# First loads on one queue, modulation columns by halves of the output, eleven GpSimd normalising steps and a new written-out order, in a block of local attention and a token-mixing MLP

## The chip, the core and the metric

The program runs on one core of a Trainium2 chip. The core has five engines that work side by side and meet through semaphores: TensorE (PE, with its weight loads PEld), VectorE (DVE), ScalarE (ACT), GpSimd (POOL) and SyncE (SP, which here only issues transfers). Sixteen DMA engines move the data. The metric is the device time of one execution in microseconds; lower is better.

## The reference

The input x has 2048 tokens of 512 features, in bfloat16. Six vectors of 512 come out of a small modulation product, and two residual branches use them:

```
mod = silu(c) @ w_mod                       # w_mod: 512 x (6*512)
sa, ca, ga, sb, cb, gb = the six slices of mod
h = layernorm(x) * (1 + ca) + sa
q, k, v = h @ wqkv                          # 32 heads of 16
# each token attends to 8 tokens: itself and 2, 4, ... 14 tokens back
attn = softmax(q . k[s - 2w] * 0.25, w = 0..7)
x = x + ga * ((attn-weighted v) @ wo)
h = layernorm(x) * (1 + cb) + sb
u = gelu(layernorm(h)^T @ w1 + b1)          # mixes along the 2048 tokens, 1792 hidden
x = x + gb * (u @ w2 + b2)^T
```

## The kernel before, in words

Tokens are worked in four chunks of 512 (`build_chunk(ch)`, line 546), each of four tiles of 128 tokens. For a chunk the program takes the row statistics of x (`ln1s`, helper `stats`, line 350), their reciprocal root (`rstd1`, line 360), a helper column -mean/std (`nb1`, `negmean`, line 374) and the normalised rows (`ln1n`, `norm`, line 380). TensorE transposes these into PSUM (`tr`, line 576) and an eviction that multiplies by 1+ca and adds sa writes the transposed activations (`hT`, line 583). Three projections follow (`qkvq`, `qkvk`, `qkvv`, line 608) with their evictions (`evq`, `evk`, `evv`).

The attention of a chunk is elementwise work on VectorE: four products of q with shifted k (`qk`, 4096 columns each, line 651), summed per head on TensorE (`red`), a maximum (`max`), its subtraction on TensorE (`sub`), the exponential on ScalarE (`exp`), the sum over the window on TensorE (`sum`), its reciprocal on ScalarE (`rb`), the scaling on VectorE (`smul`), the spreading of the weights to all lanes on TensorE (`a2`, evicted by `a2ev`), four products of the weights with shifted v (`pv`, 4096 columns each, line 726) and their sums on TensorE (`pvacc`, line 736). The shifted copies of v are made by transfers inside SBUF (`vd`, eight for each half of the head features, into the tiles vD). Then come the output projection (`wo`), its eviction with the residual (`x1ev`), sums of squares (`x1sq`), `rstd2`, `nb2`, the second normalisation (`t`), two VectorE steps with 1+cb and sb (`aff`), the third normalisation (`ln3s`, `rstd3`, `nb3`, `h3`). Where `x1ev` of a tile is on ScalarE, its `wo` has a fifth matmul that adds the residual (line 763).

The MLP's first product runs over tokens. Its first half (tiles 0 to 7) is accumulated in `mlp1_0_..` as those tiles come ready and parked in SBUF (`park0`); the second half is `mlp1_1_..`, joined by `gadd`, `gelu` and `gbm`. The second product (`mlp2`, line 917) gives the output tiles, each finished by one VectorE addition (`fin`) and one store (`st_out`). The last tile, 15, is done in two pieces of 256 columns.

Several steps may run on more than one engine: `add_any` (line 112) holds the alternatives. Which one is taken, and the order of all steps, is written out by hand in the string `ORDER` (line 27): `ln1n4:a` means that step on ScalarE, `:v` on VectorE; a digit is one of the four PSUM slots of two banks each. `schedule` (line 147) reads the string and only refuses an order that breaks a dependency. The numbers beside the alternatives are not read by it. Each engine runs its steps strictly in that order, and so does the SP queue its transfers.

The beginning, which the change touches: `ld_c` (1 KB) and `ld_wmodA` are issued by ScalarE, and `ld_x00`, `ld_x02`, `ld_wmodB`, `ld_x1`, `ld_w1a` and the rest by SP. `ld_wmodA` and `ld_wmodB` (lines 404 and 406) bring the first 1024 columns of w_mod, each for half of the 512 input features, in rows of 2 KB. `silu` is one ScalarE exponential and three VectorE steps (lines 454 to 461). `modcols0` and `modcols1` (line 472) make columns sa and ca, each over half of the inputs, so that both halves of the weights are needed for any column; `modcols_h` and `modcols_cp` add them. `warm0` to `warm4` are matmuls on the identity with no use but to keep TensorE working (line 463, counts in `WARM`, line 246).

Of the kernel before, what the change touches and what calls it, by code (L numbers as in the profile page):

```python
# [13 lines left out]
P = 128  # L14
# [13 lines left out]
consts ld_x00 ld_c consts2 warm2:0 ld_x02 ld_wmodA ld_wmodB act_table ld_x1 warm4:1 ld_w1a ld_w1b ln1s0:v ld_x2 cps:2  # L28
warm0:3 ld_w0 silu_exp ln1s1:a silu_dve halo0 ln1s2:v ln1s3:v rstd1_0_0 modcols0:0 ld_w2 nb1_0_0 rstd1_0_2 warm3:1
ln1n0:v modcols_h ln1n1:a nb1_0_2 ln1n3:v modcols1 ln1n2:v ld_wo1 tr0_00:2 tr0_02 ld_wmod5 modcols_cp tr0_10:3 hT0_0:v  # L30
tr0_12 ln1s7:a warm1:1 hT0_2:v hT0_1:v ld_x3 hT0_3:v qkvk0_0:0 ln1s6:a ln1s5:v qkvk0_0b qkvk0_2:2 ld_wmod2 ln1s4:v
evk0_0:a sc_rep rstd1_1_0 ln1s10:v ld_wo2 qkvk0_1:1 evk0_2:a ld_wo3 nb1_1_0 ln1s11:v qkvq0_0:3 ln1n5:a ln1n7:v
qkvq0_2:0 ln1s8:v evk0_1:a ln1n4:a khalo1 ln1s9:v ld_b1 evq0_0:a ln1n6:v rstd1_2_0 ld_wmod4 qk0_0 tr1_10:2 evq0_2:a
ld_wmod3 tr1_00:1 qkvq0_1:3 hT1_2:a ld_wo0 hT1_0:a qkvv0_0:0 nb1_2_0 qk0_2 hT1_3:a evq0_1:a hT1_1:a qkvv0_2:2 evv0_0:a
qk0_1 ln1n10:a qkvq1_0:3 evv0_2:a ln1n8:v ln1s15:a vd0_020 qk0_3 qkvk1_0:1 vd0_001 vd0_011 evq1_0:a red0_0:0 vd0_021
evk1_0:a ln1s12:v red0_1 vd0_000 red0_2 ln1s14:a ln1n11:v vhalo1 red0_3 qk1_0 vd0_131 qkvk1_2:2 vd0_010 ln1n9:a
vd0_121 ln1s13:a vd0_030 qkvq1_2:3 max0 ld_b2 evk1_2:a qk1_1 sub0 evq1_2:a qkvv1_0:1 khalo2 vd0_031 exp0 vd0_101 qk1_2
rstd1_3_0 vd0_111 sum0 tr2_00:2 vd0_130 rb0 red1_0:3 hT2_0:a vd0_120 red1_1 nb1_3_0 smul0 vd0_110 evv1_0:a red1_2
qk1_3 a2_0:0 vd0_100 hT2_1:a tr2_10:1 a2ev0:a qkvv1_2:2 hT2_2:a pv0_0 ln1n14:a red1_3 hT2_3:a modrows:0 ln1n13:a
qkvq2_0:1 pv0_1 mrow_ev evv1_2:a bc0 ln1n12:a biascols:0 vd1_130 pvacc0_0:2 biascols_cp ln1n15:a max1 pvacc0_1 vd1_021  # L40
evq2_0:a vd1_100 tr3_00:0 pv0_3 vd1_010 sub1 oev0_1:a qkvv2_0:1 vd1_011 exp1 vd1_020 vd1_030 pv0_2 hT3_0:a sum1
vd1_000 qkvk2_0:2 evv2_0:a vd1_001 hT3_1:a vd1_031 gmul rb1 vd1_110 pvacc0_2:1 evk2_0:a pvacc0_3 vd1_120 tr3_10:0
# [5 lines left out]
vd2_131 x1ev7:a vd2_121 ln3s0_0:v red2_0:1 x1sq4 red2_1 vd2_031 ln3s0_2:v red2_2 vd2_111 x1sq7 red2_3 ln3s0_1:v
vd2_001 qkvv3_0:0 x1ev6:a max2 vd2_101 rstd3_0_0 x1sq6 ld_w1_0_0 nb3_0_0 qk3_1 sub2 evv3_0:a qkvq3_2:2 rstd2_1_0 exp2
nb2_1_0 qkvv3_2:3 h3_2:v h3_3:v t7:a h3_1:v h3_0:v t6:a qk3_0 qkvk3_2:0 t5:a ld_w1_0_6 t4:a evv3_2:a sum2 aff1_0 rb2  # L50
red3_0:3 vd3_011 evq3_2:a mlp1_0_10_0:1 vd3_030 vd2_110 evk3_2:a mlp1_0_11_0 smul2 vd3_010 ln3s1_3:a ln3s1_1:v
mlp1_0_30_0:2 ld_w1_0_2 vd2_100 ln3s1_0:v red3_1 ln3s1_2:a vd2_130 mlp1_0_31_0 qk3_2 vd3_031 a2_2:0 vd3_000 rstd3_1_0
vd3_021 a2ev2:a nb3_1_0 vd3_020 red3_2 qk3_3 vd3_001 h3_5:a mlp1_0_00_0:0 h3_7:a mlp1_0_01_0 h3_6:a h3_4:v pv2_0
red3_3 mlp1_0_11_4 mlp1_0_10_4 max3 vd3_120 mlp1_0_31_4 park0_1:a mlp1_0_01_4 pv2_1 sub3 pvacc2_0:1 exp3 mlp1_0_00_4
pv2_2 vd3_101 sum3 vd3_100 pvacc2_1 rb3 vd3_121 mlp1_0_30_4 oev2_1:a vd3_130 smul3 mlp1_0_60_0:3 park0_3:a vd3_110
pv2_3 a2_3:1 ld_w1_0_4 pvacc2_2:2 vd3_111 a2ev3:a mlp1_0_61_0 vd3_131 pv3_0 ld_w1_1_5 pvacc2_3 mlp1_0_60_4 oev2_3:a
ld_w1_0_5 mlp1_0_61_4 park0_0:a pv3_1 wo9:1 park0_6:a wo10:2 wo11:0 x1ev9:v ld_w1_1_3 x1ev10:v wo8:3 x1sq9 x1ev11:v
# [173 lines left out]
def kernel(  # L231
# [35 lines left out]
    def T(shape, dtype, name):  # L267
        return sb.tile(shape, dtype, name=name)
# [695 lines left out]
```

## Time and profile before

| | |
|---|---|
| median of three runs | 200.23 us (200.03 to 200.43) |
| the profiled execution's own time | 199.6 us |
| its span, first to last instruction | 197.9 us |
| TensorE busy | 190.3 us, 1270 matmuls |
| VectorE busy | 156.5 us |
| ScalarE busy | 125.7 us |
| GpSimd busy | 4.3 us, all in the first 6 us |
| granted TensorE clock | 1.00 in every stage |
| DMA, mean | 170 GB/s, 33.58 MB |

All steps are recorded through one helper (line 183), so that rows of the profile are told apart by the tiles that they write and read: `prod`, `gT` and `h` written from `q_sb,k_c` are the `qk` products, `pvb` from `a2sb,vD` the `pv` products, `ps` from `pvb,stack` is `pvacc`, `ps` from `prod,group` is `red`. Times in rows are microseconds from the start of the span, then the duration; where a row ends with `x4` it is four instructions of a kind, from the start of the first to the end of the last. A duration holds the latency too, so that two neighbours on an engine start closer together than one duration; the distance of starts is called the pitch here.

### The profile page before, as it was taken

Reading aid. Unit: us, or ns where it says so; the run is one execution under the profiler, and the core shown is the slowest. Engines: PE = TensorE matmul, PEld = TensorE weight load, DVE = VectorE, ACT = ScalarE, POOL = GpSimd, SP = SyncE. Lnnn points to the kernel's source line nnn. Section 1 sums busy time; section 2 is a strip of 40 time slices with the busy share of each in tenths; the row PEclk is TensorE's granted clock in tenths of the full one; section 3 lists DMA queues with packets and bytes.
Section 4 is the critical chain, followed back from the end, with each engine's and each line's share of the span. In section 5 each row is a group of like instructions: output and inputs, shape, how many; then the busy total and the mean of one; then the engine's idle time right before and its main releaser. Section 6 shows DMA issues by size and latency. Waiting matters only on the chain.

```text
span 197.9 us, 3368 instructions
## 1 busy us (share of the span) xinstructions
PE 190.3 (96%) x1270; PEld 89.4 (45%) x1292; DVE 156.5 (79%) x209; ACT 125.7 (64%) x243; POOL 4.3 (2%) x30
## 2 busy tenths in 40 slices
PE   7999999999999999979999999999999999999994
PEld 2656545444444445424434444444444444444452
DVE  1899999999999999999999999946894515261554
ACT  3799999999999999994777999934732000000000
POOL 7100000000000000000000000000000000000000
DMA  5999965547972589696499999998000069000212
GB/s 189 364 337 325 262 148 123 165 109 177 168 126 50 161 231 230 199 216 139 109 198 271 293 284 296 288 296 227 3 0 0 27 183 297 27 27 27 83 50 82
DMA packets 45331, 33.58 MB, mean 170 GB/s; under 512 B 5252, under 2 KB 42756, under 8 KB 45316
## 3 DMA queue, kind: packets, MB, share of 16 engines
q1 hardware_dynamic: 45036, 32.85, 65.5%
q10 hardware_dynamic: 280, 0.53, 0.7%
q8 instruction: 10, 0.16, 0.4%
q14 instruction: 5, 0.04, 0.1%
HBM read 22.03 MB, written 2.10 MB: 122 GB/s over the span
## 4 chain that ended last, share of the span: by engine, by line
PE 54%; ACT 6%; DVE 4%; DMA 2%; issue 1%
PE ps L183 54%; DVE h L183 2%; DMA vD<-v_c 2%; ACT junk L183 2%; ACT h L183 1%; DVE gT L183 1%; ACT v_c L183 1%; DVE pvb L183 1%; ACT ee L183 1%; ACT a2sb L183 0%; ACT k_c L183 0%; ACT q_sb L183 0%; ACT lv L183 0%; DVE k_c L183 0%; ACT rb L183 0%
## 5 line engine op out<-in xcount | busy, mean ns | idle before, releaser
L183 DVE TENSOR_TENSOR pvb<-a2sb,vD 128x4096 bf16<-128x4096 bf16 x16 | 36.1, 2286 | 0.1
L183 PE MATMUL ps<-h,wst 128*128 128x512 bf16 x123 | 29.0, 379 | 0.6 <-ACT a2sb L183 0.2
L183 DVE TENSOR_TENSOR prod<-q_sb,k_c 128x4096 bf16<-128x4096 bf16 x9 | 20.5, 2287 | 0.3 <-ACT q_sb L183 0.3
L183 PEld LDWEIGHTS <-wst 128*128 128x128 bf16 x128 | 12.0, 98 | 16.6 <-issue 3.2
L183 PE MATMUL ps<-gT,vD 128*128 128x512 bf16 x83 | 19.1, 379 | 0.1
L183 DVE TENSOR_TENSOR q_sb<-ps,q_sb 128x512 bf16<-128x512 f32 x8 | 5.5, 688 | 14.2 <-PE ps L183 13.7
L183 PE MATMUL ps<-woq,o_sb 128*128 128x512 bf16 x61 | 15.3, 379 | 0.2
L183 PE MATMUL ps<-hTb,w_q 128*128 128x512 bf16 x63 | 15.1, 379 | 0.1
L183 PE MATMUL ps<-hTb,w_v 128*128 128x512 bf16 x60 | 14.8, 380 | 0.3
L183 PE MATMUL ps<-hTb,w_k 128*128 128x512 bf16 x62 | 14.9, 380 | 0.1
L183 PEld LDWEIGHTS <-w_q 128*128 128x128 bf16 x96 | 10.2, 108 | 10.6 <-issue 0.8
L183 PEld LDWEIGHTS <-o_sb 128*128 128x128 bf16 x106 | 10.2, 98 | 9.9 <-ACT o_sb L183 0.3
L183 DVE TENSOR_TENSOR k_c<-ps,k_c 128x512 bf16<-128x512 f32 (+1 forms) x9 | 5.6, 629 | 11.0 <-PE ps L183 11.0
L183 PEld LDWEIGHTS <-vD 128*128 128x128 bf16 x116 | 9.3, 97 | 10.4
L183 PEld LDWEIGHTS <-w_v 128*128 128x128 bf16 x80 | 8.5, 111 | 9.5 <-issue 2.3
L183 PE MATMUL ps<-gT,pvb 128*128 128x512 bf16 x53 | 12.6, 379 | 0.2
L183 ACT ACTIVATE junk<-xx,su 128x512 bf16<-128x512 bf16 x16 | 11.6, 722 | 1.6 <-DVE xx L183 1.3
L183 PEld LDWEIGHTS <-w_k 128*128 128x128 bf16 x80 | 8.5, 111 | 8.9 <-issue 1.3
L183 PE MATMUL ps<-gT,prod 128*128 128x512 bf16 x55 | 12.4, 379 | 0.1
L183 ACT ACTIVATE gT<-n_sb,b1col 128x512 bf16<-128x512 f32 x8 | 5.3, 714 | 7.7 <-DVE n_sb L183 7.7
L183 PEld LDWEIGHTS <-ident 128*128 128x128 bf16 (+1 forms) x75 | 6.4, 103 | 7.6 <-issue 2.4
L183 DVE BATCH_NORM_STATS2 st<-xx 128x6 f32<-128x512 bf16 x10 | 6.8, 680 | 3.8 <-DMA xx<-in_A_x_dram 3.8
(109 smaller groups left out, 318.5 us busy)
## 6 DMA issues: line engine op xcount, KB each, us to landing
vD<-v_c SPq DMA_DIRECT2D x64, 131.5 KB, 4.6
wst<-in_B_w_dram SPq DMA_DIRECT2D x8, 512.0 KB, 5.7
vD<-in_B_w_dram SPq DMA_DIRECT2D x3, 896.0 KB, 8.3
wst<-in_w_mod_dram SPq DMA_DIRECT2D x4, 512.0 KB, 10.1
prod<-in_B_w_dram SPq DMA_DIRECT2D x2, 896.0 KB, 8.9
pvb<-in_B_w_dram SPq DMA_DIRECT2D x2, 896.0 KB, 10.1
xx<-in_A_x_dram SPq DMA_DIRECT2D x3, 512.0 KB, 8.5
w_q<-in_B_w_dram SPq DMA_DIRECT2D x2, 512.0 KB, 5.0
```

Source lines behind the costliest of these rows:

```text
L183: r = fn(*a, **k)
```

## The change

It has seven parts.

1. First loads. The modulation weights come as four transfers, all on SP right behind the two loads of x: `ld_wmodA1`, `ld_wmodA0`, `ld_wmodB1`, `ld_wmodB0`, each for all 512 inputs and 256 output columns, in rows of 512 bytes. ScalarE issues a 1 KB load from w_mod into a tile `touch` that nothing reads. `ld_x1` is split in two and stands between the halves of the key weights; `ld_x3` and `ld_b2` move ahead of `ld_w2`.
2. Modulation columns. `modcols0` and `modcols1` each make half of the output columns over all inputs. `modcp0` and `modcp1` copy them out. Transposes are paired so that a PSUM slot holds feature tiles kp and kp+2, and `hT` of tiles 0 and 1 needs only the first half of the columns.
3. `silu` becomes three ScalarE steps (exponential, logarithm of 1 plus it, exponential) and one VectorE product.
4. `WARM` goes from (8, 6, 4, 4, 3) to (4, 4, 2, 3, 3).
5. Eleven normalising steps move to GpSimd: `ln1n6`, `ln1n4`, `ln1n8`, `ln1n11`, `t5`, `t4`, `t7`, `h3_3`, `h3_1`, `h3_11`, `h3_8`. Seven of them were on VectorE; `ln1n4`, `t5`, `t4` and `t7` were on ScalarE.
6. `ORDER` is new throughout, and other steps change between ScalarE and VectorE (among them `hT0_1` to ScalarE, `hT1_1`, `ln1s13`, `h3_6` to VectorE, `h3_2`, `h3_4` and `x1ev11` to ScalarE).
7. The last output tile is cut into 384 and 128 columns.

```
-    WARM=(8, 6, 4, 4, 3),
+    WARM=(4, 4, 2, 3, 3),
...
     def norm(dst, src, rs_ap, nb_ap, reads, nbkey, writes, name, mean_ap=None):
...
         alts = [("dve", _ts4(D, 2), f_dve),
                 ("act", _act(D, 2, False), lambda: nc.scalar.activation(dst, src, ACT.Identity, scale=rs_ap,
-                                                                        bias=nb_ap))]
+                                                                        bias=nb_ap)),
+                ("pool", 0.78, lambda: nc.gpsimd.tensor_scalar(dst, src, rs_ap, nb_ap, op0=ALU.mult, op1=ALU.add))]
...
+    dma(touch[:], w_mod.rearrange("(a b) n -> a b n", b=D // 16)[:, 0, 0:32], 1024, [], ["touch"], "ld_touch", "act")
...
-    dma(wmodA[:, 0:2, :], wmod_view[:, 0:2, 0:2 * D], 2 * D * P * 2 * 2, [], vdk[0][4:], "ld_wmodA", "act")
     G.head = [o.idx for o in G.ops if o.name.startswith("ld_x0")]
-    dma(wmodA[:, 2:4, :], wmod_view[:, 2:4, 0:2 * D], 2 * D * P * 2 * 2, [], vdk[0][:4], "ld_wmodB")
+    for hf in range(2):
+        for v in (1, 0):
+            c0 = v * D + hf * (D // 2)
+            z = 4 - 4 * hf + 2 * v
+            dma(wmodA[:, :, c0:c0 + D // 2], wmod_view[:, :, c0:c0 + D // 2], D * P * 4, [], vdk[0][z:z + 2],
+                f"ld_wmod{'AB'[hf]}{v}")
...
+        for (a, z) in ((0, 2), (2, TPC)) if ch == 1 else ((0, TPC),):
+            dma(xx[:, ch * TPC + a:ch * TPC + z, :], x_view[:, ch * TPC + a:ch * TPC + z, :], (z - a) * P * D * 2, [],
+                [("xx", ch * TPC + i) for i in range(a, z)], f"ld_x{ch}" + ("ab"[a // 2] if ch == 1 else ""))
...
+    def f_sig():
+        nc.scalar.activation(ecol[:], bank(sl_c, 0)[:, 0:KT], ACT.Exp, scale=-1.0)
+        nc.scalar.activation(ecol[:], ecol[:], ACT.Ln, bias=1.0)
+        nc.scalar.activation(ecol[:], ecol[:], ACT.Exp, scale=-1.0)
...
-                for dt_ in range(KT):
-                    for kt in (2 * kh, 2 * kh + 1):
+                for dt_ in (2 * kh, 2 * kh + 1):
+                    for kt in range(KT):
...
+        def f_cp(kh=kh):
+            pm = bank(sl_m, kh)
+            nc.vector.tensor_copy(sacol[:, 2 * kh:2 * kh + 2], pm[:, 2 * kh:2 * kh + 2])
+            nc.vector.tensor_scalar(a1col[:, 2 * kh:2 * kh + 2], pm[:, KT + 2 * kh:KT + 2 * kh + 2], 1.0, None, op0=ALU.add)
...
-                                                n_sb[:, sl, (2 * kp + k2) * P:(2 * kp + k2 + 1) * P], ident[:])
+                                                n_sb[:, sl, (2 * k2 + kp) * P:(2 * k2 + kp + 1) * P], ident[:])
...
-            for (c0, c1) in ([(0, D)] if st < NST - 1 else [(0, D // 2), (D // 2, D)]):
+            for (c0, c1) in ([(0, D)] if st < NST - 1 else [(0, 3 * P), (3 * P, D)]):
```

The pieces of the new order that the prediction speaks of:

```
+silu_exp ln1s0:v ld_w1a ln1s1:a ld_x1a silu_dve ln1s2:v halo0 ld_w1b warm2:3 ld_x1b ln1s3:v rstd1_0_0 ld_x2 modcols0:0
+ld_w0 rstd1_0_2 nb1_0_0 warm3:1 ln1n0:v ld_x3 ln1n1:a modcp0 nb1_0_2 ln1n2:v modcols1 ln1n3:v ld_b2 tr0_00:2 tr0_10:3
+modcp1 tr0_02 sc_rep ld_w2 tr0_12 hT0_0:v warm4:1 hT0_1:a hT0_2:v ld_wo0 ln1s4:a hT0_3:v qkvk0_0:0 ld_wmod2 ln1s7:v
...
+nb1_1_0 ln1s9:v ld_wo3 ln1n6:g ln1n5:a qkvq0_2:1 ln1s10:v evq0_1:a ln1n4:g evk0_2:a qk0_1 ln1n7:a qkvq0_0:3 evk0_0:a
...
+red0_0:3 ln1s13:v ln1n8:g vd0_120 red0_1 evk1_0:a ln1s12:v red0_2 vd0_130 ln1n11:g ln1n10:a red0_3 vd0_021 qk1_0
...
+biascols:0 qkvk3_2:3 ln3s0_2:v vd2_130 rstd2_1_0 ln3s0_0:a nb2_1_0 vd2_020 ln3s0_1:v t5:g qkvq3_2:2 ln3s0_3:v vd2_031
+t4:g t6:a max2 ld_w1_0_2 t7:g evk3_2:a aff1_0 evq3_2:a sub2 qkvv3_2:3 rstd3_0_0 exp2 nb3_0_0 biascols_cp h3_2:a h3_3:g
+sum2 ln3s1_2:v qkvv3_0:2 rb2 h3_1:g ln3s1_3:v ln3s1_0:a h3_0:v smul2 mlp1_0_10_0:0 ld_w1_0_6 qk3_0 evv3_0:a
```

More of the change, by code (lines that the diff above doesn't have):

```diff
@@ L27 @@
 ORDER = """
[L28 to L42, printed above, removed]
@@ L48 @@
[L48 to L57, printed above, removed]
@@ new lines @@
+tr1_10:2 evq0_0:a khalo1 tr1_00:0 hT1_1:v evq0_2:a qkvv0_2:3 ld_wmod3 qk0_0 ld_wmod5 hT1_0:a hT1_3:a qkvv0_0:1 hT1_2:a
+qk0_2 evv0_2:a qkvq1_0:2 evv0_0:a ln1s14:a qk0_3 vd0_131 qkvk1_0:0 vd0_030 vd0_011 rstd1_2_0 evq1_0:a vd0_020 nb1_2_0
+red0_0:3 ln1s13:v ln1n8:g vd0_120 red0_1 evk1_0:a ln1s12:v red0_2 vd0_130 ln1n11:g ln1n10:a red0_3 vd0_021 qk1_0
+qkvq1_2:1 ln1s15:a vd0_001 vd0_000 vd0_010 ln1n9:a qkvk1_2:2 max0 vd0_031 rstd1_3_0 vhalo1 evq1_2:a qk1_1 sub0
+qkvv1_0:0 evk1_2:a exp0 khalo2 qk1_3 vd0_110 tr2_00:1 evv1_0:a sum0 vd0_100 tr2_10:2 rb0 vd0_121 qkvv1_2:0 hT2_0:a
@@ new lines @@
+red3_3 pv2_0 mlp1_0_31_4 mlp1_0_11_4 max3 mlp1_0_10_4 vd3_120 vd3_110 mlp1_0_01_4 park0_1:a pv2_1 vd3_020 sub3 bc3
+pvacc2_0:0 exp3 mlp1_0_30_4 pv2_2 vd3_131 sum3 vd3_011 pvacc2_1 rb3 mlp1_0_00_4 vd3_111 oev2_1:a vd3_121 smul3
+mlp1_0_60_0:3 park0_0:a vd3_130 pv2_3 a2_3:0 vd3_100 mlp1_0_61_0 a2ev3:a vd3_101 ld_w1_0_4 pvacc2_2:2 ld_w1_1_0
+pvacc2_3 pv3_0 mlp1_0_60_4 oev2_3:a mlp1_0_61_4 park0_3:a wo11:0 pv3_1 park0_6:a ld_w1_0_5 wo8:2 x1ev11:a wo10:1
+ld_w1_1_3 x1ev8:v wo9:3 x1ev10:v x1sq8 pvacc3_0:0 ld_w1_1_1 x1sq11 x1ev9:v pvacc3_1 pv3_2 x1sq10 mlp1_0_20_0:2 x1sq9
```

96 lines of the change are left out of this document (46 added, 50 removed).

## The prediction

> **What bounds the kernel now.** I read the page first, then the chain that ended last, then the rows of TensorE and VectorE in the stretches that the chain names, and last the first 17 us.
>
> ```profile
> span 197.9 us, 3368 instructions
> PE 190.3 (96%) x1270; PEld 89.4 (45%) x1292; DVE 156.5 (79%) x209; ACT 125.7 (64%) x243; POOL 4.3 (2%) x30
> PE   7999999999999999979999999999999999999994
> DVE  1899999999999999999999999946894515261554
> ```
>
> The chain (start, length, what) and, behind it, rows of TensorE and VectorE (start, length; in brackets the idle time before and who ended it):
>
> ```profile
> 87.03 0.92 ACT a2sb L183
> ...
> 127.02 10.74 PE ps L183 x49
> ...
> 190.27 4.73 PE ps L183 x28
> ...
> 195.02 0.42 DVE k_c L183
> ```
>
> ```profile
> 64.27 0.62 PE L183 MATMUL ps<-pvb,stack 128*32 128x512 bf16 x8 [0.31 <-DVE pvb L183]
> ...
> 87.16 0.61 PE L183 MATMUL ps<-gT,group 128*32 128x512 bf16 x8 [0.90 <-DVE gT L183]
> ...
> 98.00 6.75 DVE L183 TENSOR_TENSOR pvb<-a2sb,vD 128x4096 bf16<-128x4096 bf16 x3
> ...
> 100.55 0.62 PE L183 MATMUL ps<-pvb,stack 128*32 128x512 bf16 x8
> ```
>
> In the page's slices each digit is a fortieth of the span, 4.9 us, in tenths. From the chain's last ScalarE piece at 87.03 on there is only TensorE, at 219 ns a matmul (10.74 us for 49), to its last matmul near 195.0; then one 0.42 us addition and the last store. VectorE stands at nine tenths or more from the third slice to about 128 us. TensorE looks as full, but its small idle times before 100 us name VectorE products (0.31 and 0.90 us above): it keeps step with VectorE there and only afterwards has a backlog. The hand-over is the last `pv` product of chunk 2, the first of the three that start at 98.00; its `pvacc2_3` starts at 100.55. What lies on TensorE behind it is fixed work. So the end moves with (a) the time at which VectorE finishes that product and (b) TensorE work added behind it. (a) is the time of VectorE's first `qk` product plus the VectorE work between the two plus its waits.
>
> **The start.**
>
> ```profile
> 1.42 3.17 PE L183 MATMUL ps<-ident 128*128 128x512 bf16 x7 [1.42 <-POOL onecol L183]
> ...
> 1.79 0.47 SPq L183 DMA_DIRECT2D vD<-in_w_mod_dram  x1
> ...
> 4.63 2.33 PE L183 MATMUL ps<-ident 128*128 128x512 bf16 x8
> ...
> 8.06 0.54 PE L183 MATMUL ps<-sc,vD 128*128 128x1 bf16 x16
> ...
> 8.47 1.05 PE L183 MATMUL ps<-ident,n_sb 128*128 128x128 bf16 x16
> ...
> 9.07 0.63 ACT L183 ACTIVATE junk<-xx 128x512 bf16<-128x512 bf16 x1 [0.62 <-DMA xx<-in_A_x_dram]
> ...
> 9.11 1.90 DVE L183 TENSOR_SCALAR hTb<-ps,a1col,sacol 128x512 bf16<-128x512 bf16 x4 [0.24 <-PE ps L183]
> ...
> 10.65 3.62 PE L183 MATMUL ps<-hTb,w_k 128*128 128x512 bf16 x15
> 10.68 0.63 ACT L183 ACTIVATE junk<-xx 128x512 bf16<-128x512 bf16 x1
> ...
> 12.15 0.58 ACT L183 ACTIVATE k_c<-ps 128x512 bf16<-128x512 f32 x1
> 12.66 0.48 ACT L183 ACTIVATE lv<-mv,epscol 128x2 f32<-128x2 f32 x2
> ...
> 14.36 0.80 ACT L183 ACTIVATE n_sb<-xx,nb,rs 128x512 bf16<-128x512 bf16 x1
> 15.07 0.58 ACT L183 ACTIVATE k_c<-ps 128x512 bf16<-128x512 f32 x1
> ...
> 16.25 0.59 ACT L183 ACTIVATE q_sb<-ps 128x512 bf16<-128x512 f32 x1
> ...
> 16.94 2.29 DVE L183 TENSOR_TENSOR prod<-q_sb,k_c 128x4096 bf16<-128x4096 bf16 x1 [0.31 <-ACT q_sb L183]
> ```
>
> The load of the second weight half (KB, us from issue to landing), and two 5 us windows, whose last two columns are the DMA engines' share and GB/s:
>
> ```profile
> vD<-in_w_mod_dram SPq DMA_DIRECT2D x1, 512.0 KB, 5.7
> ```
>
> ```profile
> 5.00:10.00 5.00, 5.00 (x63) 3.15 (x62) 4.34 (x16) 4.00 (x13) 0.64 (x10) 1.00 1.06 363
> 110.00:115.00 5.00, 5.00 (x36) 2.05 (x35) 4.73 (x4) 4.40 (x7) 0.00 (x0) 1.00 1.18 292
> ```
>
> Now the second weight half lands at 1.79 + 5.7 = 7.5, its columns start at 8.06, the transposes at 8.47, the projections at 10.65 (after four VectorE evictions, 9.11 to 11.0), and the first `qk` product at 16.94, right behind ScalarE's q eviction (16.25 + 0.59).
>
> *Weights.* The changed queue moves the same 1.5 MB (x, then weights) before the second half is complete, in rows of 512 bytes. The 110 to 115 window moves only w1 and w2, whose rows are 512 bytes, at 292 GB/s with the engines full; the 5 to 10 window, rows of 1 and 2 KB, 363. 1.05 MB takes 3.6 us at 292 and 2.9 at 363, so the second half lands between 7.5 and 8.2. I take 7.9: the narrow rows cost, while x no longer shares the engines with the other queue. Nothing is gained below 7.5: tr waits for `ln1n3` on VectorE until about 8 as well. `ld_touch` adds one issue on ScalarE where `ld_wmodA`'s goes away: nothing; no row prices its effect on later loads, so it stays inside these ends.
>
> *To the projections.* Weights 7.9, columns 8.1, transposes 0.41 later (8.06 to 8.47) at 8.5, through at 9.6. `hT0_0` and `hT0_1` then run on two engines, `hT0_1` on ScalarE from 9.65 for 0.8 us (the normalising row, 0.80), so projections start at 10.5 instead of 10.65. `silu` goes earlier (four cold warm-ups, 0.45 us each by the first row, instead of seven before `cps`) and costs ScalarE two short steps more and VectorE two less; the weights cover it until 7.9, and without that cover it would cost ScalarE some 0.3 us.
>
> *To the first product.* ScalarE then does `hT0_1` 0.7 (pitch), two statistics pairs 3.2 (9.07 to 10.68 is 1.61 each), the reciprocal root 0.65, an eviction 0.5 (12.15 to 12.66), one normalising 0.7 (14.36 to 15.07) and `evq0_1` 0.6: the first product starts at 9.65 + 6.35 = 16.0, which is 0.94 earlier. The other queue entries moved past fit: w0 lands 2.1 MB after the weights, 7.9 + 5.8 = 13.7, needed by TensorE 16 matmuls after 10.5, at 14.0; w2, behind `ld_x3`, 3.1 MB, 16.6 at 363 GB/s, needed at about 18.
>
> **VectorE between the two products.**
>
> ```profile
> 23.63 0.41 DVE L183 TENSOR_SCALAR n_sb<-xx,mv,rs 128x512 bf16<-128x512 bf16 x1
> 23.95 2.29 DVE L183 TENSOR_TENSOR h<-q_sb,k_c 128x4096 bf16<-128x4096 bf16 x1
> 26.15 0.69 DVE L183 BATCH_NORM_STATS2 st<-xx 128x6 f32<-128x512 bf16 x1
> ...
> 26.98 0.38 DVE L183 TENSOR_SCALAR n_sb<-xx,mv,rs 128x512 bf16<-128x512 bf16 x1
> ```
>
> Groups of one form (count, busy us, mean ns, idle before):
>
> ```profile
> L183 DVE TENSOR_REDUCE nm<-ps 128x128 bf16<-128x1024 f32 x4 | 4.9, 1214 | 0.0
> L183 POOL MEMSET pvb<- 128x1024 bf16 x1 | 1.0, 951 | 0.0
> L183 POOL TENSOR_SCALAR_AFFINE_SELECT stack<-stack 128x32 bf16<-128x32 bf16 x4 | 0.8, 212 | 0.3
> L183 POOL TENSOR_SCALAR_AFFINE_SELECT ident<-ident 128x128 bf16<-128x128 bf16 x1 | 0.3, 292 | 0.1
> ```
>
> Leaving VectorE here: `ln1n8`, `ln1n11`, `h3_3`, `h3_1` to GpSimd, `h3_2`, `h3_4` to ScalarE; coming: `h3_6`. Net five at a pitch of 0.32 (23.63 to 23.95), -1.6. Coming also `ln1s13` at 0.83 (26.15 to 26.98) and `hT1_1` at 0.46 (1.90 us for four). Other swaps are even. Sum -0.3. ScalarE loses more in the same stretch (a statistics pair, `hT1_1`, three `t`, against two `h3` more: about 1.6 + 0.7 + 2.1 - 0.7 = 3.7 us); I credit that nothing, since VectorE is full.
>
> One wait is added: `tr2_00`, 8 transposes, 0.5 us by the row of 16, now stands on TensorE before `sum0`; `rb0` and `smul0` wait behind it. By the pitches `smul0` would come up on VectorE about 0.4 before `rb0` is ready: +0.4.
>
> *GpSimd steps.* No row shows one. Half of the 1024-column memset is 0.48; the two selects differ by 80 ns for 96 columns, so one of 512 would take 0.61; with two operations per element instead of one, 0.21 + 2 x 0.4 = 1.0. Ends 0.48 and 1.0; I take 0.75, nearer the select. Each group follows a `nb` step, and VectorE then runs work that is no product: two statistics (1.66) beside two steps in chunk 1 and again in chunk 2, two statistics and the maximum (2.8, with the reduce row less its 0.08 of overlap) beside `t5 t4 t7`, two statistics and a copy (1.8) beside `h3_3 h3_1`. With 0.2 us to start, 1.7, 1.7, 2.45 and 1.7 us fit to 0.1. Cost nothing; without cover, the price is the rival below. `h3_11`, `h3_8` come when TensorE has a backlog.
>
> **TensorE behind it, and the end.** `x1ev11` on ScalarE adds the residual matmul, +0.22. Tile 15 in 384 and 128 columns has the same columns; the smaller last addition gains about 0.1, and `st_out14` now stands just before the last store on SP, whose issue takes 0.47: together 0, ends -0.1 and +0.3. Sixteen warm-ups instead of 25 lie before the projections: nothing while TensorE waits there anyway.
>
> **Sum.** -0.94 - 0.3 + 0.4 + 0.22 = -0.6. The profiled execution took 199.6, so 199.0; it lies 0.6 below the median of the runs, 200.23, against which the result is told: 199.6. With the weights at 7.5 the sum would be -1.0, with them at 8.2 it would be -0.3.
>
> **Rivals.**
>
> *More is freed (198.6).* The chain before 88 us runs on ScalarE from about 75. If it is ScalarE's 3.7 us that holds VectorE and TensorE, `rb0` is not late and the 0.4 disappears, and of the 0.3 and 0.9 us waits above about half go too: -1.6. Against it: VectorE shows no idle there.
>
> *The start gives nothing (200.2).* Weights at 8.2 by the 292 GB/s row, or w0 after 14.0, and then `tr` and ScalarE's list begin 0.3 later, and 0.1 is lost on the first matmuls of q: about -0.1.
>
> *GpSimd excludes VectorE (201.6).* The other side. A GpSimd step that runs over its cover holds up the `qk` product or `aff` behind it, or waits a whole 2.2 us product for it. At 1.0 us a step the four groups take 2.2, 2.2, 3.2 and 2.2 us, overrunning by 0.55 + 0.55 + 0.4 + 0.4 = 1.9: -0.6 + 1.9 = +1.3. It turns a gain into a loss from 0.86 us a step (nine steps times 0.11 less the 0.4 of slack). For it: nothing measured says these steps are short. The Trainium skill (SBUF — State Buffer, Who interferes with whom) says that a VectorE instruction with two SBUF inputs and a reading GpSimd instruction never run together, and that the later one waits out the whole of the earlier; by that rule it would be this case. No run here shows it, since POOL is idle after 6 us.
>
> *TensorE falls back (201.7).* With fewer warm-ups TensorE has gaps while it waits for the weights. Cold matmuls took 0.45 us (first row, seven in 3.17), warm ones 0.22; the cold stretch lasted from 1.42 to about 4.6. Another 3.2 us at half speed in the projections costs 1.6, and is lost only in part to the other waits: +1.5. The Trainium skill (TensorE: Matmul & The Clock Gate, Part 1) puts the window after which an idle array slows at about 3.4 us; the expected gaps are under 1 us, so it speaks against this rival.
>
> **How the numbers follow.** Forecast 0.37, more freed 0.17, start gives nothing 0.16, GpSimd excludes 0.22, clock 0.08. A measurement here tells about 0.2%, 0.4 us. The first two are faster: 0.54; the third is within 0.2%: 0.16; the last two are slower: 0.30. Range 198.4 to 201.6 leaves out the far side of the first rival (weights at 7.5 with all waits gone) and of the last. The forecast's own range is 199.0 to 199.9.
>
> **What would show it.** Right: the first `qk` product from 15.7 to 16.3, transposes from 8.3 to 8.8, the last `pv` product of chunk 2 from 96.9 to 97.5, GpSimd rows of 0.6 to 0.85 us, VectorE with no idle over 0.3 but at `smul0`. Wrong: a `qk` row longer than 2.3 us or an idle before one while GpSimd runs; matmul pitches of 0.4 after 9 us; w0 or w2 named as releaser; TensorE idle after 100 us.

## The result, and the profile after

The changed kernel takes 200.66 us (median of 21 executions, 199.47 to 202.30), the kernel before 199.96 in the same comparison (21 executions, 199.58 to 200.56). The ratio is 1.0041, 95% interval 1.0022 to 1.0061: slower by 0.4%, where 0.3% less than the then known 200.23 was forecast. The profiled execution took 200.35, with a span of 198.3.

First, busy times and the granted clock from the page of the changed kernel; the clock line was at full speed throughout before.

```profile
span 198.3 us, 3360 instructions
...
PE 189.5 (96%) x1261; PEld 89.5 (45%) x1284; DVE 154.4 (78%) x201; ACT 124.7 (63%) x241; POOL 12.6 (6%) x41
...
PEclk9879999999999999999999999999999999999999
```

The clock line has 8 and 7 in the second and third slices (5 to 15 us). TensorE's rows in the timeline of the changed kernel show what happened there:

```profile
5.78 0.35 PE L184 MATMUL ps<-sc,vD 128*128 128x1 bf16 x8
6.67 0.35 PE L184 MATMUL ps<-sc,vD 128*128 128x1 bf16 x8 [0.54 <-DMA vD<-in_w_mod_dram]
6.88 0.81 PE L184 MATMUL ps<-ident 128*128 128x512 bf16 x3
7.57 0.35 PE L184 MATMUL ps<-sc,vD 128*128 128x1 bf16 x8
8.45 0.35 PE L184 MATMUL ps<-sc,vD 128*128 128x1 bf16 x8 [0.53 <-DMA vD<-in_w_mod_dram]
8.67 1.82 PE L184 MATMUL ps<-ident,n_sb 128*128 128x128 bf16 x16
10.28 1.48 PE L184 MATMUL ps<-ident 128*128 128x512 bf16 x3
11.56 1.76 PE L184 MATMUL ps<-hTb,w_k 128*128 128x512 bf16 x5
```

The four weight pieces arrive one after the other, and before the second and the fourth TensorE stands idle half a microsecond. Right behind, the 16 transposes take 1.82 us instead of 1.05, three warm-ups 1.48, and the projections start at 11.56 instead of 10.65. Two rows of the stage table (columns as before: stretch, busy times of the engines, granted clock, share of the DMA engines, GB/s) show two things that differ:

```profile
4.00:5.00 1.00, 1.00 (x3) 0.30 (x2) 0.97 (x4) 0.97 (x4) 0.99 (x2) 1.00 1.00 279
...
9.00:10.00 1.00, 1.00 (x12) 1.00 (x11) 0.20 (x3) 0.00 (x0) 0.00 (x0) 0.50 1.10 347
```

The same stretch of the kernel before:

```profile
4.00:5.00 1.00, 1.00 (x4) 0.23 (x3) 0.70 (x3) 0.27 (x2) 0.99 (x2) 1.00 1.06 401
```

From 4 to 5 us the loads move 279 GB/s instead of 401, and from 9 to 12 us TensorE runs at half its clock (0.50 in each of the three rows). The last weight piece, issued at 3.41, lands at 8.41. What follows on ScalarE and VectorE, and the end, in the timeline of the changed kernel:

```profile
10.52 0.78 ACT L184 ACTIVATE hTb<-ps,sacol,a1col 128x512 bf16<-128x512 bf16 x1 [2.93 <-PE ps L184]
...
16.38 0.60 ACT L184 ACTIVATE q_sb<-ps 128x512 bf16<-128x512 f32 x1
...
17.08 2.29 DVE L184 TENSOR_TENSOR prod<-q_sb,k_c 128x4096 bf16<-128x4096 bf16 x1 [0.16 <-POOL n_sb L184]
...
26.97 1.52 POOL L184 TENSOR_SCALAR n_sb<-xx,rs,nb 128x512 bf16<-128x512 bf16 x2 [9.96 <-PE ps L184]
...
28.25 2.37 DVE L184 TENSOR_TENSOR prod<-q_sb,k_c 128x4096 bf16<-128x4096 bf16 x1
...
71.59 2.29 DVE L184 TENSOR_TENSOR prod<-q_sb,k_c 128x4096 bf16<-128x4096 bf16 x1
...
75.12 2.27 POOL L184 TENSOR_SCALAR h<-xx,rs,nb 128x512 bf16<-128x512 bf16 x3 [46.64 <-DVE nb L184]
...
82.80 2.29 DVE L184 TENSOR_TENSOR prod<-q_sb,k_c 128x4096 bf16<-128x4096 bf16 x1
...
98.14 2.28 DVE L184 TENSOR_TENSOR pvb<-a2sb,vD 128x4096 bf16<-128x4096 bf16 x1
...
193.75 1.38 PE L184 MATMUL ps<-gT,o_sb 128*128 128x512 bf16 x16
...
194.56 0.90 DVE L184 TENSOR_TENSOR k_c<-ps,k_c 128x512 bf16<-128x512 f32 x2
```

ScalarE begins its list (`hT0_1` first) at 10.52, when the transposes are through, and the first `qk` product follows its q eviction. It starts at 17.08, not at 16.0 (before: 16.94); the last `pv` product of chunk 2 at 98.14 (before: 98.00); TensorE ends at 195.13 (before: the row below, 194.98).

```profile
192.86 2.12 PE L183 MATMUL ps<-gT,o_sb 128*128 128x512 bf16 x16
```

The bracket at 17.08 names GpSimd as the releaser, but the product stands 0.10 behind the end of the q eviction here (16.98) as before the change (16.84, then 16.94) and as in the run `nogpsimd` below, which has no GpSimd step there (17.35, then 17.45). So it waited for ScalarE.

So in these two executions the distance from the first product to the last `pv` product of chunk 2 is 81.06 in both, and from there to the end of TensorE 96.99 against 96.98. What lies behind the start came out even; the start came out 1.1 us later than forecast. And there is a part that no row shows: the time lies 2.01 to 2.10 us above the span in all 21 executions, against 1.66 to 1.76 in 29 executions of the kernel before beside the first experiments. The median span is 198.6, against some 198.25 before (199.96 less 1.71): half of the 0.7 us lies inside the span, and half outside.

The executions of the changed kernel fall into groups by their mean granted clock: seven at 0.999 or 1.000 (median 200.14), ten at 0.991 (200.72), four at 0.981 (202.13). At half speed, 0.009 of 198 us is 3.6 us of slow clock, and 0.019 is 7.5: none, one or two slow stretches of some 3.6 us.

### The profile page after: what moved, and what is told of

It is laid out like the page before. It is cut to its first block, busy times and chain, and to the rows that moved or that the text cites. A ratio compares the mean times of both kernels' runs of the same rounds, so it can differ in the third digit from the quotient of the medians.

```text
span 198.3 us, 3360 instructions
## 1 busy us (share of the span) xinstructions
PE 189.5 (96%) x1261; PEld 89.5 (45%) x1284; DVE 154.4 (78%) x201; ACT 124.7 (63%) x241; POOL 12.6 (6%) x41
## 4 chain that ended last, share of the span: by engine, by line
PE 61%; ACT 24%; DVE 4%; issue 4%; DMA 3%; SPq 1%; DVEq 0%; ACTq 0%
PE ps L184 61%; ACT junk L184 6%; DMA vD<-in_w_mod_dram 3%; ACT hTb L184 2%; ACT xx L184 2%; DVE pvb L184 2%; ACT o_sb L184 2%; ACT v_c L184 2%; DVE h L184 1%; ACT h L184 1%; ACT n_sb L184 1%; ACT k_c L184 1%; ACT q_sb L184 1%; SPq L184 1%; ACT ee L184 1%
## 5 line engine op out<-in xcount | busy, mean ns | idle before, releaser
L184 PE MATMUL ps<-h,wst 128*128 128x512 bf16 x123 | 28.5, 379 | 0.4 <-issue 0.2
L184 DVE TENSOR_TENSOR k_c<-ps,k_c 128x512 bf16<-128x512 f32 (+2 forms) x9 | 5.5, 629 | 14.3 <-PE ps L184 14.3
L184 PEld LDWEIGHTS <-o_sb 128*128 128x128 bf16 x106 | 9.7, 98 | 10.5 <-issue 0.4
L184 ACT ACTIVATE hTb<-ps,sacol,a1col 128x512 bf16<-128x512 bf16 x12 | 8.9, 787 | 2.9 <-PE ps L184 2.9
L184 DVE BATCH_NORM_STATS2 st<-xx 128x6 f32<-128x512 bf16 x11 | 7.4, 672 | 3.7 <-DMA xx<-in_A_x_dram 3.7
```

The source lines that it names most:

```text
L184: r = fn(*a, **k)
```

## The experiments

All are compared with the kernel before, run on the same chip beside them. "Outside" is the time less the span.

**The clock.** `fill` puts matmuls into idle gaps of the changed kernel, three between the two halves of each `modcols` step:

```
+                if v == 1:
+                    for _ in range(3):
+                        nc.tensor.matmul(pm[:, P:4 * P], lhsT=ident[:], rhs=ident[:].unsqueeze(1).to_broadcast([P, 3, P]), ...)
```

> The changed kernel with three matmuls on the identity (384 columns each) put into modcols0 and into modcols1, between the eight columns of each first weight piece and the eight of each second. Theory 1 (TensorE lost its clock because it stood idle twice 0.54 us before the second pieces, with 0.5 us more ahead of modcols1): the granted clock is 1.00 in every slice, the 16 transposes take 1.05 us instead of 1.82, the projections start at 10.5 instead of 11.56, the first qk product at 16.1 instead of 17.08, and the time falls by about 0.8 us from 200.66 to 199.9, with no run far above 200.6. Rival A (the four late weight pieces set the start, the clock hides under them): clock 1.00, but the first qk product stays above 16.7 and the time within 0.3 us of 200.66. Rival B (it is the fewer warm-ups before 5 us): slices still under 1.00, transposes 1.8 us.

Measured: 200.09 (199.84 to 200.79), ratio 0.9996 (0.9977 to 1.0014), and no execution with a mean clock under 0.998. TensorE's rows:

```profile
9.27 0.35 PE L184 MATMUL ps<-sc,vD 128*128 128x1 bf16 x8
9.49 1.05 PE L184 MATMUL ps<-ident,n_sb 128*128 128x128 bf16 x16
...
11.03 3.28 PE L184 MATMUL ps<-hTb,w_k 128*128 128x512 bf16 x12
```

The transposes are back at 1.05, and the long executions are gone. The median fell by 0.57. But in the profiled execution the weights landed later than in the one above (the last piece at 9.23 instead of 8.41), so the transposes begin at 9.49 and its first product stands at 17.07: Theory 1 was right on the clock, and rival A on what remains behind it.

`fewwarm` turns it round: the kernel before with the changed counts alone.

```
-    WARM=(8, 6, 4, 4, 3),
+    WARM=(4, 4, 2, 3, 3),
```

> The kernel before with the changed kernel's warm-up counts (4, 4, 2, 3, 3 instead of 8, 6, 4, 4, 3) and nothing else. Its two weight loads are complete at 6.6 to 7.5 us, so TensorE stands idle once for about 1.3 us ahead of modcols0 and for some 0.3 us ahead of modcols1. Theory 1 (idle time of TensorE between 5 and 9 us costs the clock): transposes or projections at half speed (1.5 us or more for the 16 transposes), some runs 1 to 2 us above their median, median 0.4 us or more above the kernel before. Rival (it takes the four gaps of the late pieces): transposes 1.05 us, time within 0.2 us of before.

Measured: 200.81 (199.38 to 202.04), ratio 1.0045 (1.0021 to 1.0068).

```profile
6.17 0.55 PE L183 MATMUL ps<-sc,vD 128*128 128x1 bf16 x16 [0.64 <-DVE st L183]
6.58 0.81 PE L183 MATMUL ps<-ident 128*128 128x512 bf16 x3
8.02 0.55 PE L183 MATMUL ps<-sc,vD 128*128 128x1 bf16 x16 [0.64 <-DMA vD<-in_w_mod_dram]
8.44 1.74 PE L183 MATMUL ps<-ident,n_sb 128*128 128x128 bf16 x16
9.96 1.91 PE L183 MATMUL ps<-ident 128*128 128x512 bf16 x4
```

Two gaps of 0.64 us, with an old start otherwise, and the transposes take 1.74. One small edit of the change loses the clock by itself and costs 0.9 us. All of that lies inside the span (median 199.1 against 198.2), where the changed kernel lost only 0.35 of its 0.7, so the mechanism is shown, and that the two losses come out alike in size is chance. It also shows that no gap longer than that is needed. Gaps of this length don't always cost the clock: the profiled execution of `g4` below, with the changed kernel's start, has three of 0.51, 0.69 and 0.51 us at the same places, and its transposes take 1.05; that of `fill` stands idle for 1.22 us ahead of its first columns. What decides between the executions isn't shown.

The recorded clock doesn't catch every long execution: three of `fewwarm` took 201.75 to 202.04 at 1.000, and three of the 29 of the kernel before beside the first experiments 201.23 to 201.52 at 0.999 or more.

**The loads.** `startback` gives the changed kernel the old first loads, modulation columns and warm-up counts; silu, order, GpSimd steps and tail stay changed.

```
-    (four loads ld_wmodA1, A0, B1, B0 on SP; ld_touch; columns by halves of the outputs; WARM=(4, 4, 2, 3, 3))
+    dma(wmodA[:, 0:2, :], wmod_view[:, 0:2, 0:2 * D], ..., "ld_wmodA", "act")
+    dma(wmodA[:, 2:4, :], wmod_view[:, 2:4, 0:2 * D], ..., "ld_wmodB")
+    WARM=(8, 6, 4, 4, 3)
```

> The changed kernel with the first weight loads, the modulation columns and the warm-up counts as before (two loads of 512 KB in 2 KB rows on two queues, no touch, columns by halves of the inputs, 25 warm-ups); silu, order, GpSimd steps and tail as changed. Theory (the loss sits in the new start): weights complete at 7.5 us instead of 8.4, clock 1.00, projections at 10.5, first qk product near 16.0 to 16.3, time 199.7. Rival (the loss sits in the new order behind it): first qk product earlier, and still 200.4 or more.

Measured: 199.63 (199.39 to 201.09), ratio 0.9988 (0.9965 to 1.0011); first product at 16.39, last `pv` product of chunk 2 at 97.42. The loss sat in the new start; with the old one the rest of the change is as fast as the kernel before or a little faster, though its time outside the span is 2.07. Its first product is 0.55 earlier than before the change with the same loads, columns and warm-ups, so what the start gains there comes from the rest of the change (order, engines, `silu`), not from the new loads. Its columns stood behind warm-ups, so two more runs trimmed these:

```
-    WARM=(8, 6, 4, 4, 3),
+    WARM=(4, 8, 2, 4, 3),    # start_trim
+    WARM=(4, 6, 2, 2, 3),    # start_trim2
```

> The kernel of the run startback with 21 warm-ups instead of 25: four ahead of the transposition of c instead of eight, ten behind it. There modcols0 started at 7.14, with its weights there at 6.6 and twelve warm-ups counted ahead of it. Theory (the start was then bound by warm-ups and by the late silu): first columns at 6.6, first qk product 0.3 us or so earlier than 16.39, clock 1.00, time 199.3. Rival (VectorE's statistics and ln1n3, or the second half of the weights, set the transposes): within 0.1 us of 199.63.

> The kernel of the run start_trim with two warm-ups fewer ahead of modcols0 and two fewer between modcols0 and modcols1 (17 instead of 21). There the first weights had landed at 6.0 and their columns started at 7.22, behind warm-ups. Theory (warm-ups are still what the columns wait for): columns at 6.5 and 7.7, transposes at 8.2 to 8.5 (ln1n3 ends at 8.6), first qk product at 16.0, clock kept, time 0.2 to 0.3 us less than 199.31. Rival (four warm-ups fewer open idle time): some runs lose the clock, transposes 1.7 us, median 199.6 or more.

`start_trim`: 199.31 (198.90 to 200.56), ratio 0.9955 (0.9931 to 0.9979). The time is the expected one, the way to it is not: in the profiled execution the columns start at 7.22 (`startback`: 7.14) and the first product at 16.34, only 0.05 earlier. `start_trim2`: 199.09 (198.70 to 199.28), ratio 0.9945 (0.9927 to 0.9962), the fastest version here, below both kernels (median span 197.05). Its rows:

```profile
5.92 0.55 PE L184 MATMUL ps<-sc,vD 128*128 128x1 bf16 x16
...
8.30 0.55 PE L184 MATMUL ps<-sc,vD 128*128 128x1 bf16 x16 [1.36 <-DMA vD<-in_w_mod_dram]
8.71 1.05 PE L184 MATMUL ps<-ident,n_sb 128*128 128x128 bf16 x16
...
16.17 2.29 DVE L184 TENSOR_TENSOR prod<-q_sb,k_c 128x4096 bf16<-128x4096 bf16 x1
```

The clock held here beside a wait of 1.36 us, longer than the gaps that cost it above. The six executions all kept it; whether more would is open.

Which half of the new loading made the weights late, the one queue or the rows of 512 bytes? `widesp` takes `start_trim` and puts both wide loads on SP; `fill2q` takes `fill` and puts the first two narrow pieces on ScalarE's queue.

```
-    dma(wmodA[:, 0:2, :], ..., "ld_wmodA", "act")
+    dma(wmodA[:, 0:2, :], ..., "ld_wmodA")                              # widesp
...
-                f"ld_wmod{'AB'[hf]}{v}")
+                f"ld_wmod{'AB'[hf]}{v}", "sp" if hf else "act")         # fill2q, both ahead of act_table
```

> The kernel of the run start_trim with both weight loads (512 KB each, rows of 2 KB) issued by SP behind the two of x, so that one queue carries all first loads, as in the changed kernel, but in wide rows. Theory (the 512 byte rows delay the weights, not the one queue): modcols0 and modcols1 start no later than in start_trim (7.22 and 8.48), transposes by 9.0, time within 0.2 us of 199.3. Rival (the one queue delays them): second columns at 8.9 or later, time 199.7 or more.

> The kernel of the run fill (no lost clock) with the first two weight pieces issued by ScalarE, on its own queue, ahead of its table load; rows stay 512 bytes. Theory 1 (the one queue makes the weights late, since they wait for x): the pieces land earlier by 0.5 to 1 us, first qk product near 16.4, time 199.6. Rival (the 512 byte rows make them late): last piece no earlier than 8.2, time within 0.2 us of 200.09.

`widesp`: 200.26 (199.30 to 200.91), ratio 1.0013 (0.9999 to 1.0027), apart from `start_trim`'s interval. The stage table and TensorE's first columns of `widesp`:

```profile
4.00:5.00 1.00, 1.00 (x3) 0.30 (x2) 0.96 (x4) 0.97 (x4) 0.99 (x2) 1.00 0.63 135
```

```profile
8.25 0.55 PE L184 MATMUL ps<-sc,vD 128*128 128x1 bf16 x16 [0.59 <-DMA vD<-in_w_mod_dram]
...
9.66 0.55 PE L184 MATMUL ps<-sc,vD 128*128 128x1 bf16 x16
```

and the stage table of `start_trim`:

```profile
4.00:5.00 1.00, 1.00 (x3) 0.30 (x2) 0.49 (x3) 0.97 (x4) 0.99 (x2) 1.00 1.06 401
```

With one queue the DMA engines were 63% busy from 4 to 5 us and moved 135 GB/s, with two they were full and moved 401; the first columns came at 8.25 instead of 7.22. My theory (the narrow rows) fell: the one queue is what costs, 0.6% by the two ratios. All profiled executions agree: from 4 to 5 us the DMA engines moved 135 to 279 GB/s in the seven that have x and these weights on one queue, 389 to 406 in the nine with the wide halves on two. And on one queue the narrow pieces were all there between 8.41 and 9.23 (six executions), the wide halves of `widesp` at 9.61. The Trainium skill (DMA: Bandwidth & Descriptors, Issuing engines are not separate DMA queues) says that issuing from several engines saves only the time of issuing; in this stretch the traces show more than that: `widesp` issues the first half 0.4 us later (at 1.80 instead of 1.43), and its columns start 1.0 later. `fill2q` gave 203.20, ratio 1.0153 (1.0119 to 1.0188), 238 GB/s from 4 to 5 us and last columns at 10.69: two queues don't help narrow pieces whose first two were to come first. All six of its executions lost the clock as well (0.983 to 0.992, the transposes 1.87), in spite of the added matmuls, so its time isn't the price of the loads alone. So the two hang together, and what narrow rows cost on two queues isn't separated.

`fillnotouch` removes `ld_touch` from `fill` (`-    dma(touch[:], w_mod..., "ld_touch", "act")`).

> The kernel of the run fill without the 1 KB load from w_mod that ScalarE issues first. Theory (it does nothing): time within 0.2 us of 200.09. Rivals: it opens the way for the weights, so that without it the first piece lands 0.3 us or more later and the time rises; or it stands in the way, and the time falls by as much.

Measured: 199.87, ratio 0.9988 (0.9971 to 1.0006), 0.2 us from `fill` with overlapping intervals: no effect that can be told.

**The tail.** `tail256`: `-[(0, 3 * P), (3 * P, D)]  +[(0, D // 2), (D // 2, D)]`.

> The changed kernel with its last output tile cut into 256 and 256 columns again, in the changed order. Theory (the last addition queues behind fin14, and its store behind the issue of st_out14): from the end of the last matmul to the end of the span 0.25 us less than now (3.2 us now, 2.9 before), time 200.4. Rival: the store's landing ends it either way, within 0.1 us of now.

Measured: 200.67, ratio 1.0030 (1.0000 to 1.0060), median as the changed kernel. From the last matmul's end to the end of the span 3.1 us, 3.2 in the changed kernel, 2.9 before. Rival right; the tail isn't where the time went. Its profiled execution has all 16 transposes at half speed (1.87 us) beside a granted clock of 1.00 in the table, so the clock column alone doesn't clear a stage.

**The GpSimd steps.** `nogpsimd` puts the eleven back, `g4` leaves only the four of chunks 1 and 2.

```
-ln1n6:g ln1n4:g ln1n8:g ln1n11:g t5:g t4:g t7:g h3_3:g h3_1:g h3_11:g h3_8:g
+ln1n6:v ln1n4:a ln1n8:v ln1n11:v t5:a t4:a t7:a h3_3:v h3_1:v h3_11:v h3_8:v     # g4: the first four stay :g
```

> The changed kernel with its eleven GpSimd steps back on the engines that they had before (seven on VectorE at a pitch of 0.32 us, four on ScalarE). Theory (they cost VectorE nothing but 0.25 us of touches): slower than the changed kernel by up to 1.2 us (four VectorE steps before the last pv product of chunk 2 are 1.3 us, one has a gap to fill). Rival (GpSimd's shared use holds VectorE up somewhere): as fast or faster, at most 200.6, and the qk row of 2.37 us is 2.29 again.

> The changed kernel with only the four GpSimd steps of chunks 1 and 2 (ln1n6, ln1n4, ln1n8, ln1n11); t5, t4, t7, h3_3, h3_1, h3_11, h3_8 back on their engines of before. Theory (0.03 us a step outside the span): difference of time and span 1.87. Rival (all or nothing): 2.06, or 1.75 as without any. The time shows where the 3.4 us of the run nogpsimd lie: if behind t4, t5, t7 on ScalarE, which then sets the maximum and the third normalisation of chunk 2, it is 203 or more; if in chunks 1 and 2, about 201.5.

`nogpsimd`: 204.10, ratio 1.0197 (1.0152 to 1.0242); `g4`: 203.64, ratio 1.0177 (1.0153 to 1.0200). VectorE's rows of `nogpsimd`:

```profile
72.62 2.29 DVE L184 TENSOR_TENSOR prod<-q_sb,k_c 128x4096 bf16<-128x4096 bf16 x1
...
80.18 1.23 DVE L184 TENSOR_TENSOR h<-h,ab_bc 128x2048 bf16<-128x2048 bf16 x1 [1.40 <-ACT h L184]
...
86.33 2.29 DVE L184 TENSOR_TENSOR prod<-q_sb,k_c 128x4096 bf16<-128x4096 bf16 x1
```

Between these two products lie 13.71 us, in the changed kernel 11.21: `aff` waits 1.40 for `t` on ScalarE, and two `h3` are back on VectorE. `g4`, whose steps in this stretch are also back, has 13.79. So in the new order the three `t` and two `h3` here are worth about 2.5 us, twice what my theory had allowed for all eleven; it had counted VectorE's steps and not the wait for ScalarE. In both runs TensorE also waits 0.81 and 1.67 us in this stretch and loses its clock behind that (in `g4` eight matmuls take 3.44 us, in the changed kernel 1.89), so their times hold some of that too. In the old order the seven VectorE steps alone gain nothing on GpSimd; the `t` stay on ScalarE there, as `g7` moves only those seven (`-ln1n6:v ... h3_8:v  +ln1n6:g ... h3_8:g` in the kernel before).

> The kernel before with seven normalising steps moved from VectorE to GpSimd (ln1n6, ln1n8, ln1n11, h3_3, h3_1, h3_11, h3_8), in the order of before: this part of the change alone. Theory on the time outside the span (0.03 us for each GpSimd step that waits on other engines): difference of time and span 1.93. Rival (the new order, not the steps): 1.71 to 1.76. On VectorE: five steps at a pitch of 0.32 leave it before the last product of chunk 2, so that this starts up to 1.6 us earlier if nothing waits for GpSimd (time 198.7); but in this order products stand close behind the steps, and in the run g33 a step that met a product took 4.4 us, so ln1n11 and h3_1 may come some 2 to 4 us late. Then transposes of chunk 2 or the first half of the MLP wait, and the time is 200 or more.

Measured: 199.92, ratio 1.0001 (0.9978 to 1.0023), outside 1.72 to 1.78.

```profile
19.55 2.29 DVE L183 TENSOR_TENSOR gT<-q_sb,k_c 128x4096 bf16<-128x4096 bf16 x1
19.80 6.92 POOL L183 TENSOR_SCALAR n_sb<-xx,rs,nb 128x512 bf16<-128x512 bf16 x1 [4.77 <-issue]
...
21.75 2.29 DVE L183 TENSOR_TENSOR prod<-q_sb,k_c 128x4096 bf16<-128x4096 bf16 x1
23.95 2.29 DVE L183 TENSOR_TENSOR h<-q_sb,k_c 128x4096 bf16<-128x4096 bf16 x1
...
77.13 0.80 DVE L183 TENSOR_SCALAR h<-h,mv,rs 128x512 bf16<-128x512 bf16 x1
```

A GpSimd step of 0.77 us that met a product took 6.92, through three products in a row, and these kept their 2.29 us and their pitch of 2.20. At 77.13, between products, the waiting GpSimd work got its turn and a VectorE step of 0.38 took 0.80; another 0.15 at a time went into `nb` steps and into waits for ScalarE. The distance from the first product to the last `pv` product of chunk 2 became 81.27, 0.2 more than before.

**Outside the span.** `oneg` has one GpSimd step (`-h3_11:v  +h3_11:g`), `g33` and `g11` have idle ones:

```
+        for _ in range(33):                                             # g11: 11, of 128 x 512
+            nc.gpsimd.tensor_scalar(gjunk[:], ident[:, 0:32], onecol[:, 0:1], epscol[:, 0:1], op0=ALU.mult, op1=ALU.add)
```

> The kernel before with a single step on GpSimd, h3_11, which comes at about 116 us, where TensorE has a backlog. The runs so far have a time that lies 2.00 to 2.12 us above the span wherever a kernel has GpSimd steps, and 1.66 to 1.76 where it has none. Theory (any late use of GpSimd adds 0.35 us outside the span): time 200.3, span as before, difference 2.0 or more. Rival A (it grows with the number of steps, 0.03 us each): difference 1.74. Rival B (something else of the new order makes it): difference 1.7.

> The kernel before with 33 steps on GpSimd in a row at about 121 us, each on 128 x 32 values into a tile that nothing reads: extra work off every path, beside TensorE's backlog. The run with one step had its time 1.74 us above its span, the kernel before 1.71, those with eleven 2.06. Theory (each GpSimd step adds 0.03 us outside the span, whatever its size): difference 2.7 us, time 1.0 us above before. Rival A (it goes by the time that GpSimd works, 0.04 us for each us): difference 1.8 to 1.9. Rival B (it is not the steps as such): 1.71.

> The kernel before with eleven steps of 128 x 512 in a row on GpSimd at about 121 us, into a tile that nothing reads. Theory (0.03 us a step outside the span): difference of time and span 2.06, time 0.35 us above before. Rival (the difference needs the steps' waits on other engines, which these lack): 1.71 to 1.75, time as before. Either way VectorE's statistics and normalising near 121 us keep their lengths if the two engines don't hold each other up.

Times: `oneg` 200.34, ratio 1.0016 (0.9993 to 1.0040); `g33` 199.78, 0.9994 (0.9984 to 1.0004); `g11` 199.91, 1.0005 (0.9992 to 1.0018). Outside, medians: `oneg` 1.74, `g33` 1.75, `g11` 1.84, `g7` 1.76, `g4` 1.97, `nogpsimd` 1.75, changed kernel 2.06. So the 0.35 us come with the GpSimd steps of the changed kernel, 0.2 of them with the four of `g4`, but not with their number (33 small ones or seven in the old order cost nothing), and neither of my theories stands. It stays open. The idle steps ran from 5.7 us on, since nothing held them back to 121, and that made `g33` a test of something else. Its rows:

```profile
19.27 2.31 DVE L183 TENSOR_TENSOR gT<-q_sb,k_c 128x4096 bf16<-128x4096 bf16 x1
19.54 4.39 POOL L183 TENSOR_SCALAR gjunk<-ident,onecol,epscol 128x32 bf16<-128x32 bf16 x1
...
21.50 2.28 DVE L183 TENSOR_TENSOR prod<-q_sb,k_c 128x4096 bf16<-128x4096 bf16 x1
```

GpSimd was under way beside all `qk` products of chunks 0 and 1, and VectorE kept to the times of before.

## Why the prediction was wrong, point by point

- *Weights at 7.9, between 7.5 and 8.2.* Failed, and first in the chain. The term priced 1.05 MB at a full rate of 292 to 363 GB/s. With one queue the engines were not full, or moved 279: the last piece landed at 8.41 in the changed kernel, at 8.77 and 8.70 in `nogpsimd` and `g4`, at 9.23 in `fill`. The rows read for the price came from other stretches: 5 to 10 us with two queues, and 110 to 115.
- *Warm-ups nothing; TensorE falls back, chance 0.08.* Failed. The rival's mechanism happened, and `fewwarm` shows that the step "nothing while TensorE waits there anyway" is the one: 0.45% on its own, and `fill` takes about as much back (1.0041 to 0.9996). The argument against it was the Trainium skill's rule (TensorE: Matmul & The Clock Gate, Part 1) that an idle window of about 3.4 us slows the array. The traces disagree with my use of it: two gaps of half a microsecond within 2.5 us were enough in some executions. The same part says that the window runs freely, so that how many matmuls are slow at the start differs from run to run; that executions of one kernel differ in the clock lost is so here, and one lost stretch is some 3.6 us. The rival's 201.7 was too high for the median, and short of the worst, 202.30.
- *First product at 16.0.* 17.08, from these two. In this execution 0.17 of the 1.1 us is the later start of the transposes (8.67 for 8.5), 0.77 their slow clock, and 0.2 ScalarE's list (6.56 from 10.52 on, for 6.35); in `fill` it is the transposes' start, at 9.49. With the old loads and fewer warm-ups the product came at 16.17, so the steps from the weights to it, ScalarE's list among them, were about right.
- *`w0` at 13.7, needed at 14.0.* It landed at 14.43, and in `fill` at 15.20, where TensorE waits 0.29 us for it. That is one of the signs of being wrong, but the first product didn't wait for it: ScalarE's list was the later of the two.
- *VectorE between the products, -0.3 + 0.4 = +0.1.* Right within 0.1 in sum: 81.06 before and after (81.03 in `startback`). The wait at `smul0` was 0.17, not 0.4, so the steps that left VectorE saved less than 0.3 as well; that the two misses cancel is luck.
- *`x1ev11` +0.22.* The residual matmul is there (17 matmuls from 102.76 to 106.53, where 16 went from 102.83 to 106.38), but the distance to the end of TensorE grew by 0.01 only; where it was made up isn't shown.
- *Tail 0, ends -0.1 and +0.3.* 0.25 in the profiled executions, nothing in the medians.
- *GpSimd 0.75 us a step, cost nothing.* Right: 0.77, with one touch of 0.08 (the product of 2.37 at 28.25, which starts before the two steps at 26.97 are through). The rival "GpSimd excludes VectorE" (0.22) didn't come about, since the cover held, but its mechanism is real: of the two ways that it named, `g7` shows the second, with the GpSimd step waiting for three products instead of one. The Trainium skill (SBUF — State Buffer, Who interferes with whom) has the exclusion, and the trace agrees; that whoever issues first holds up the other doesn't carry to a row of products, since GpSimd, which stood ahead of the second and third, still waited for them.
- *The other rivals.* "The start gives nothing" (0.16) had the place right, with weights after 8.2 and `w0` after 14.0, and the size wrong: it took the start to be 0.1 better than before, and it was 0.14 worse in the profiled execution and more where the clock was lost. "More is freed" (0.17) fell: `startback`, with the start of before, keeps 81.03 from product to product, and `g7` shows that freed VectorE time alone buys nothing in the old order.
- *Span to time.* The sum kept the 1.7 us around the span of before. It was 2.06: another 0.35, which no step had.

Together: forecast -0.6, measured +0.7. The clock accounts for 0.6 (medians) to 0.9 (ratios), and the time outside the span for 0.35. `fill` less `startback` gives 0.46 for the loads by medians and 0.16 by ratios, and their intervals overlap. The sum is 1.4 either way (0.57 + 0.46 + 0.35 by medians, 0.9 + 0.16 + 0.35 by ratios), about the 1.3 that was missed. That the 0.35 lie outside the span is measured; why is open.

## What to carry to other kernels

Matmuls that only keep TensorE busy are part of the schedule: when loads are rearranged, recount every gap in front of the first real work, and look at the pitch of the matmuls behind it in several executions, not in one. Price early loads by the rate of the first microseconds, where a second queue may fill what one leaves empty, not by a rate from the middle of the kernel. Give work to GpSimd beside VectorE work that isn't a two-input product: a step that met three of those in a row waited them all out here.

## What the runs showed that was not expected

- The time around the span is no constant of a kernel family: 1.71 us in the kernel before and 2.06 in the changed one, within 0.1 from run to run, with a cause left open.
- A GpSimd step of 0.77 us can last 6.92 us beside back-to-back products, which themselves aren't slowed.
- Half speed of TensorE can be seen in the matmul rows (16 transposes in 1.87 us in `tail256`) where the granted clock is shown as 1.00.
- The landing of the same first loads varies by 0.8 us between profiled executions (the last weight piece at 8.41 in the changed kernel and at 9.23 in `fill`).
